# Odd tokens of two batches moved out of phase H0 and Y0, sums and kv by 64x64 quadrants, phi(q) ahead of phi(k)

## The chip, the cores and the metric

The kernel runs on one core of one Trainium2 chip. The metric is the device time of one execution in microseconds (us), taken from the runs listed below. A core has five engines that run side by side, each through its own list of instructions in order: TensorE (PE in the profile; its weight loads are shown as PEld), VectorE (DVE), ScalarE (ACT), GpSimd (POOL) and SyncE (SP). SP, ACT and POOL also start transfers (DMAs); those started by SP and ACT go through hardware queues, those started by POOL through a software queue, and all of them are carried by the same 16 DMA engines.

## What is computed

Linear attention over 8 batches, 8 heads, 576 tokens and 64 values per head, and behind it a two-layer network with a swish between its layers. Cut to what matters:

```python
def phi(x): return np.where(x > 0, x, np.exp(x) - 1.0) + 1.0
q_p, k_p = phi(q), phi(k)
kv  = np.einsum('bhsd,bhse->bhde', k_p, v)
z   = np.sum(k_p, axis=2)
num = np.einsum('bhsd,bhde->bhse', q_p, kv)
den = np.einsum('bhsd,bhd->bhs', q_p, z)[..., None] + 1e-06
x   = (num / den)            # heads put side by side: 4608 tokens x 512
h   = x @ w_in               # 512 -> 2048
g   = h / (1 + np.exp(-beta * h))
out = g @ w_out              # 2048 -> 512
```

## The kernel before

**Stages.** The order of all instructions is written out by hand; no scheduler changes it. For each block of tokens there is an H phase (h = x @ w_in, 16 column groups `ff` of four 512-column matmuls each, L395, and a Silu on ACT behind each group, L403) and a Y phase (out = g @ w_out, four row groups `t`, each of 16 matmuls in four parts `i`, L413). Phase H0/Y0 is batch 0, H1/Y1 batch 1, and so on to H7/Y7; a ninth pair, H8/Y8, takes what is left over from all batches, as follows.

**Odd tokens.** A batch has 576 tokens, held as J = 9 slices of 64. Eight slices make four blocks of 128 tokens (t = 0 to 3), which are the 512 tokens of a main phase. The ninth slice (t = 4, "odd") has 64 tokens; those of the eight batches are put side by side in `xT_tail` (512 columns), which only H8 reads, at the end of the kernel. For batches 2 to 7 the odd tokens are computed along with the others, in `numers` and `norms`. For batches 0 and 1 they have steps of their own: a transpose of their q (`q_trans` with t = 4), their denominators (`dens`, `recips`), their numerators (`numer0(b, 4)`) and a transpose of the quotient (`x_trans(b, 4, ...)`). Batch 0 has these four steps inside H0, after ff = 5, 7, 8 and 10 (L651 to L660); batch 1 has them in Y0 (L698, L703, L705), at its end (L736), and in H1 after ff = 8 (L778).

**Sums and kv of batches 0 and 1.** `row_products` (L175) multiplies a 64-row half of phi(k), all 128 columns, by a moving operand: two columns of ones for the sums z (`z_products`), 128 columns of v for kv (`kv_direct`). Half of each 128x128 product belongs to two different heads and is not wanted; `z_evac` and `kv_evac` multiply it away with a 0/1 mask while they copy it from PSUM. For batches 2 to 7 `kv_both` (L215) computes the same by 64x64 quadrants: four matmuls, one for each pair of a 64-row half and a 64-column half, that use different quarters of the array.

**Attention of batch 1.** It is worked into Y0. DVE and ACT do phi(k) first and phi(q) second (`phi_all`, L680 and L681: two exponentials on ACT, two relu steps and two minima on DVE for each). PE has Y0's parts i = 0 and 1 for all four t (32 matmuls, L682 to L684), two matmul groups more, the sums of batch 1, then the transposes of phi(q) in two lots with `y_mm` calls between them, kv, the denominators, and from L706 on the last parts of Y0 alternating with numerators and transposes.

**Loads.** POOL's queue loads, in this order: k of batch 0, v of batch 0, `w_in` (four parts), `w_out` parts 0 to 2, k of batch 1, q of batch 1, `w_out` part 3, v of batch 1, then q, k and v of batch 2 (L99 to L119, L517 to L522, L673 to L675). Batch 0's q is loaded in two halves by two hardware queues, SP's and ACT's (L93, L94). SP's queue also carries the stores of the output, the transposes made by DMA (`q_trans_dma`, `x_trans_dma`) of batches 2 to 7, and v of batches 3 to 7.

**PSUM and buffers.** `num0ps` and `miscps` have two banks each in the first part and are given up for `numps` before H1; `mmps` has four banks, which the H and Y phases turn through. phi(q) has two buffers (batch b uses the one of batch b - 2), and so has the tag `kv_bd`.

Of the kernel before, what the change touches and what calls it, by code (L numbers as in the profile page):

```python
# [8 lines left out]
F32 = mybir.dt.float32  # L9
BF16 = mybir.dt.bfloat16  # L10
ALU = mybir.AluOpType
# [5 lines left out]
def kernel(  # L17
# [72 lines left out]


    beta_row = consts.tile([FC, P], F32)
    for h0, eng in ((0, nc.sync), (2, nc.scalar)):  # L93
        load(eng, q0f, q, 0, h0, 2)  # L94
    nc.sync.dma_start(out=beta_row, in_=moe_beta.rearrange("(c p) -> c p", p=P))
    nc.vector.memset(warm, 0.5)  # L96
    tiny = consts.tile([P, 2], BF16)
    nc.scalar.activation(tiny[:, 0:1], warm[:, 0:1], ACTF.Exp)
    for h0 in (0, 2):  # L99
        load(nc.gpsimd, xk[0], k, 0, h0, 2)  # L100
# [15 lines left out]
    w_in_v = moe_w_in.rearrange("(c p) f -> p c f", p=P)  # L116
    w_out_v = moe_w_out.rearrange("(c p) m -> p c m", p=P)
    for i in range(4):
        nc.gpsimd.dma_start(out=w_in_sb[i], in_=w_in_v[:, :, i * 512 : (i + 1) * 512])  # L119

    def load_w_out(i):
        nc.gpsimd.dma_start(out=w_out_f[i], in_=w_out_v[:, i * 4 : (i + 1) * 4, :])
# [49 lines left out]
            vaug[b % 2][:, pr, :, :, 0:D], src[:, places(b, pr)].rearrange("p h j d -> p j h d")  # L172
        )

    def row_products(b, pr, dsts, mov):  # L175
        for j in range(J):
            for hh in range(2):
                r = slice(hh * G, (hh + 1) * G)
                nc.tensor.matmul(  # L179
                    dsts[hh], st[b, "k"][r, pr, j, :], mov(r, j),  # L180
                    start=(j == 0), stop=(j == J - 1), skip_group_check=True,
                )

    def z_products(b, pr, ps):

        row_products(b, pr, [a[:, 256 + 2 * pr : 258 + 2 * pr] for a in ps], lambda r, j: ones[r])

    def z_evac(ps):
        for hh in range(2):
            nc.vector.tensor_mul(  # L190
                z0[:, hh], ps[hh][:, 256:260].rearrange("p (a h) -> p a h", a=2),
                kvmask[:, :, :, 0],
            )

    def kv_direct(b, pr, ps):
        row_products(
            b, pr, [a[:, pr * P : (pr + 1) * P].rearrange("p (h d) -> p h d", h=2) for a in ps],
            lambda r, j: vb[b][r, 2 * pr : 2 * pr + 2, j, :],
        )

    def kv_evac(b, hh, prs, ps):
        p0, p1 = prs[0], prs[-1] + 1
        nc.vector.tensor_mul(
            st[b, "kv"][:, hh, p0:p1].rearrange("p a (h e) -> p a h e", h=2)[:, :, :, 0:D],
            ps[hh][:, p0 * P : p1 * P].rearrange("p (a h d) -> p a h d", a=p1 - p0, h=2),
            kvmask[:, p0:p1, :, 0:D],
        )

# [6 lines left out]
    def kv_both(b):  # L215

        t = num_tile("kvp")
        for pr in range(2):
            for j in range(J):
                for h in range(2):  # L220
                    for hh in range(2):
                        r = slice(hh * G, (hh + 1) * G)
                        c = slice(h * D, (h + 1) * D)
                        nc.tensor.matmul(  # L224
                            t[c, hh, pr * EA : (pr + 1) * EA],
                            st[b, "k"][r, pr, j, c],
                            vaug[b % 2][r, pr, j, h, 0:EA],
                            start=(j == 0), stop=(j == J - 1), skip_group_check=True,
                        )
        st[b, "kvd"] = work.tile([P, 2, 2 * EA], BF16, tag="kv_bd", name="kvd")  # L230
        nc.vector.tensor_copy(st[b, "kvd"], t[:, :, 0 : 2 * EA])  # L231

# [15 lines left out]
    def q_trans(b, ts, tp, engs):  # L248

        if (b, "qT") not in st:  # L250
            st[b, "qT"] = work.tile([P, NT, 2, 2, P], BF16, tag="qT", name="qT")
        slots = 1 if ts[0] == NT - 1 else 2
        tv = tp.rearrange("p (t a h i g) -> p t a h i g", a=2, h=2, i=slots, g=G)
        for k, t in enumerate(ts):
            for pr in range(2):
                for i in range(slots):
                    nc.tensor.matmul(  # L257
                        tv[:, k, pr, :, i, :], st[b, "q"][:, pr, 2 * t + i, :], identity,
                        is_transpose=True, start=True, stop=True, skip_group_check=True,
                    )  # L260
        for k, (t, eng) in enumerate(zip(ts, engs)):
            q_copy(b, k, t, tp, eng)

    def q_trans_dma(b):
        st[b, "qTd"] = work.tile([P, 38, G], BF16, tag="qT", name="qTd")
        nc.gpsimd.memset(st[b, "qTd"][:, 36:37], 0.0)
        for hh in range(2):
            st[b, "qTd", "dma"] = nc.sync.dma_start_transpose(
                out=st[b, "qTd"][:, hh * 2 * J : (hh + 1) * 2 * J],
                in_=st[b, "q"][hh * G : (hh + 1) * G].rearrange("p a j c -> p (a j c)"),  # L270
            )

    def q_stat(b, t, hh, pr, n):
        if (b, "qTd") in st:
# [27 lines left out]
    def numers(b):  # L302
        pairs = [num_tile("nps") for _ in range(2)]
        odd = [mm_tile("nps_m") for _ in range(2)]
        for k in range(2):
            dst = [pairs[k][:, h] for h in range(2)]
            numer_tile(b, dst, k)
            numer_tile(b, dst, 2, (k,), 4)
        numer_tile(b, odd, 3)
        for hh in range(2):  # L310
            quads(b, odd, 4 + hh, lambda c: (c, J - 1), hh, None)
        st[b, "nps"] = pairs, odd

    def xs_tile(b, t):
        st[b, "xs", t] = work.tile([P, 8, D], BF16, tag="xs", name="xs", bufs=4)
# [45 lines left out]
    def x_trans(b, t, eng):  # L361
        n = P if t < NT - 1 else G
        xv = st[b, "xs", t].rearrange("p i a d -> p (i a d)")
        if b == 1 and t == NT - 1:
            tp = num_tile("xtp")[:, 0].bitcast(BF16)[:, 0 : KC * P].rearrange(
                "p (c t) -> p c t", c=KC
            )
        else:
            tp = miscps.tile([P, KC, P], BF16, tag="misc", name="xtp")
        for p in range(KC):  # L370
            nc.tensor.matmul(  # L371
                tp[:, p, :n], xv[:n, p * P : (p + 1) * P], identity[:n, :n],
                is_transpose=True, start=True, stop=True, skip_group_check=True,
            )
        if eng is nc.scalar:
            nc.scalar.copy(x_dst(b, t), tp[:, :, :n])
        else:
            eng.tensor_copy(x_dst(b, t), tp[:, :, :n])  # L378

    def x_trans_dma(b, t):  # L380
# [4 lines left out]

        for pr in range(2):
            nc.sync.dma_start_transpose(
                out=xT_tail[:, pr:4:2, b * G : (b + 1) * G],
                in_=xv[pr * G : (pr + 1) * G, 0 : 2 * P],
            )  # L390

# [155 lines left out]
    bps = miscps.tile([P, FC], F32, tag="misc", name="bps")  # L547
    nc.tensor.matmul(bps, beta_row, ident16, is_transpose=True, start=True, stop=True)
    nc.scalar.copy(beta_s, bps)
    z_evac(zt)  # L550

    def q_trans0(t):
        q_trans(0, (t,), misc_bf()[:, 0 : 512 if t < NT - 1 else 256], (nc.scalar,))

    def numer_part(ts, pr):
        numer_norm(ts, pr, numer_mm(ts, pr))
# [55 lines left out]
    def diagonal(hh):  # L612

        for h in range(2):
            r = slice(h * D, (h + 1) * D)
            nc.scalar.copy(
                kv0[r, hh, 1, h * EA : h * EA + D], kvp0[hh][r, P + h * D : P + (h + 1) * D]
            )

    diagonal(0)  # L620
# [26 lines left out]
    for ff in range(4, FC):  # L647
        hp = mm_tile("h_ps")
        h_mm(0, xT[0], ff, hp)
        silu(0, ff, hp)  # L650
        if ff == 5:  # L651
            q_trans0(4)
        if ff == 7:
            dps4 = num0_tile()
            dens(0, (4,), dps4)
            recips(4, 5, G, dps4)
        if ff == 8:
            numer0(0, 4)
        if ff == 10:
            x_trans(0, 4, nc.vector)  # L660

    def w_out_scale(i, n_act):
        for c in range(4):
# [13 lines left out]
    for i in range(3):  # L677
        w_out_scale(i, 0)
    yps = [mm_tile("y_ps") for _ in range(4)]
    phi_all(1, "k")  # L680
    phi_all(1, "q")  # L681
    for i in range(2):  # L682
        for t in range(4):
            y_mm(0, t, i, yps[t])  # L684
    kv1 = [miscps.tile([P, 512], F32, tag="misc", name="kv1") for _ in range(2)]
    kv_tile(1)
    y_mm(0, 0, 2, yps[0])
    y_mm(0, 1, 2, yps[1])
    for pr in range(2):
        z_products(1, pr, kv1)  # L690
    z_evac(kv1)
    w_out_scale(3, 0)
    y_mm(0, 2, 2, yps[2])
    for ts in ((0, 1), (2, 3)):
        q_trans(1, ts, num0_tile().bitcast(BF16), (nc.scalar, nc.scalar))
    y_mm(0, 3, 2, yps[3])
    dps1 = num0_tile()
    q_trans(1, (4,), dps1.bitcast(BF16)[:, 512:768], (nc.scalar,))  # L698
    for pr in range(2):
        kv_direct(1, pr, kv1)  # L700
    for hh in range(2):
        kv_evac(1, hh, (0, 1), kv1)
    dens(1, range(NT), dps1)  # L703
    recips(0, 4, P, dps1)
    recips(4, 5, G, dps1)  # L705
    y_mm(0, 0, 3, yps[0])  # L706
    y_out(0, 0, yps[0], copier=nc.scalar)
    numer0(1, 0)
# [24 lines left out]
    for pr in range(2):  # L733
        phi_relu(2, "k", pr, xin(2, "k", pr))
        phi_min(2, "k", pr)
    numer0(1, 4)  # L736
    num0_pool.__exit__(None, None, None)
    misc_pool.__exit__(None, None, None)
    numps = ctx.enter_context(tc.tile_pool(name="numps", bufs=2, space=bass.MemoryType.PSUM))
# [33 lines left out]
    for b in range(1, B + 1):  # L773
        n = b + 1
        sh, sy = {}, {}
        if b == 1:
            at(sh, 0, lambda: q_trans_dma(2))
            at(sh, 8, lambda: x_trans(1, 4, nc.vector))  # L778
            at(sh, 1, lambda: [v_copy(nc.gpsimd, 2, pr) for pr in range(2)])
            at(sh, 2, lambda: load_kq(3, st[2, "qTd", "dma"]), lambda: load_v(3))  # L780
        if n < B:
            at(sh, 10, lambda: kv_both(n))
            at(sh, FC - 1, lambda: numers(n), lambda: [norms(n, k) for k in range(3)])
# [40 lines left out]
```

## Time and profile before

| what | value | from |
|---|---|---|
| median of 3 runs | 290.11 us (290.07 to 290.31) | the times |
| the profiled execution, whole | 290.31 us | the times |
| its span in the profile | 288.5 us | the page |
| PE busy | 279.8 us, 97% of the span | the page |
| ACT, DVE, POOL busy | 159.7, 107.2, 36.7 us | the page |
| H0 with 512 columns starts (L395) | 20.66 us | the chain of waits |
| Y0 starts (L413) | 32.40 us | the chain of waits |
| H1 starts | 52.16 us | the chain of waits |
| Y1, H2, Y2 start | 68.00, 81.92, 97.28 us | the chain of waits |

The profiled execution is the slowest of the three; 290.31 less 288.5, 1.8 us, lies outside the span. All moments in the text are counted from the start of the span. The chain of waits follows the work that ended last back to the start: at each step to the instruction, or the transfer, that released it. What stands in the chain sets the end; what does not stand in it was hidden behind something. A line of the timeline reads: start, duration, engine, line of the code, operation, what it writes and reads, count, and in brackets how long the engine stood idle before and what released it. PE's durations in the timeline overlap (its work is pipelined), so what a group of matmuls adds to the time is read from the chain, where the pieces do not overlap.

### The profile page before, as it was taken

How to read it: one execution, taken by the hardware profiler on the slowest of the kernel's cores; microseconds unless marked ns; L12 is line 12 of the kernel's file. 1: busy time of each engine (PE TensorE's matmuls, PEld its weight loads, DVE VectorE, ACT ScalarE, POOL GpSimd, SP SyncE). 2: the span in 40 equal slices, each digit the busy share in tenths (PEclk: the TensorE clock that was granted, in tenths of full speed). 3: DMA queues.
4: the chain of work that ended last, by engine and by line, in shares of the span. 5: the costliest groups of instructions: out<-in, count | busy, mean ns of one | idle time of the engine just before them, and what ended most of it. 6: DMA issues, size and time to landing. Idle time of an engine off the chain costs nothing.

```text
span 288.5 us, 5796 instructions
## 1 busy us (share of the span) xinstructions
PE 279.8 (97%) x2409; PEld 137.3 (48%) x2409; DVE 107.2 (37%) x261; ACT 159.7 (55%) x217; POOL 36.7 (13%) x54
## 2 busy tenths in 40 slices
PE   7799999999999999999999999999999999999994
PEld 2574457544444444444444444544454444444443
DVE  3842776825710581048103920393025100110021
ACT  4777757966647843685277628771750186028400
POOL 8632100320014000400050007000000000000000
PEclk9999999999999999999999999999999999999999
DMA  7999999599499739973898489749304410230033
GB/s 215 206 218 395 247 252 204 124 208 209 79 150 287 127 69 157 282 134 65 136 272 156 78 147 272 141 82 136 93 2 78 116 36 0 65 82 1 0 75 74
DMA packets 51083, 40.90 MB, mean 142 GB/s; under 512 B 30944, under 2 KB 42480, under 8 KB 51056
## 3 DMA queue, kind: packets, MB, share of 16 engines
q1 hardware_dynamic: 37888, 22.89, 37.0%
q0 software_dynamic: 12736, 16.91, 29.7%
q10 hardware_dynamic: 432, 0.72, 0.7%
q8 instruction: 19, 0.31, 0.4%
q14 instruction: 8, 0.07, 0.1%
HBM read 36.71 MB, written 9.44 MB: 160 GB/s over the span
## 4 chain that ended last, share of the span: by engine, by line
PE 93%; DVE 2%; DMA 2%; ACT 1%; issue 0%; DVEq 0%
PE y_ps L413 43%; PE h_ps L395 42%; DMA stage<-in_q_dram 2%; PE kvp L224 1%; PE h_ps L597 1%; PE nps L289 1%; PE kv L179 1%; DVE phi_q L153 1%; PE nps_m L289 1%; PE xtp L371 0%; PE nps L493 0%; ACT e L142 0%; DVE r L146 0%; PE tp L587 0%; PE nps L257 0%
## 5 line engine op out<-in xcount | busy, mean ns | idle before, releaser
L403 ACT ACTIVATE g<-h_ps,beta_c 128x512 bf16<-128x512 f32 x144 | 98.0, 688 | 95.9 <-PE h_ps L395 95.4
L413 PE MATMUL y_ps<-w_out,g 128*128 128x512 bf16 (+3 forms) x600 | 127.1, 371 | 0.0
L395 PE MATMUL h_ps<-xT,w_in 128*128 128x512 bf16 x496 | 110.2, 379 | 0.3 <-DVE xT L378 0.2
L413 PEld LDWEIGHTS <-g 128*128 128x128 bf16 x600 | 57.6, 98 | 64.0
L395 PEld LDWEIGHTS <-w_in 128*128 128x128 bf16 x560 | 53.9, 98 | 63.9 <-issue 0.2
L237 DVE COPY y_sb<-y_ps 128x512 f32<-128x512 f32 (+2 forms) x35 | 23.4, 672 | 73.3 <-PE y_ps L413 73.3
L231 DVE CAST kvd<-kvp 128x260 bf16<-128x260 f32 x6 | 2.6, 428 | 50.0 <-PE kvp L224 50.0
L83 POOL DMA_DIRECT2D xq<-in_q_dram x7 | 5.2, 744 | 110.5 <-ACT g L403 75.9
L142 ACT ACTIVATE e<-xk 128x1152 bf16<-128x1152 bf16 x16 | 17.7, 1149 | 0.0
L142 ACT ACTIVATE e<-xq 128x1152 bf16<-128x1152 bf16 x14 | 15.6, 1155 | 0.1
L395 PE MATMUL h_ps<-xT_tail,w_in 128*128 128x512 bf16 x64 | 14.0, 379 | 0.0
L153 DVE TENSOR_TENSOR phi_k<-e,r 128x1152 bf16<-128x1152 bf16 x16 | 11.6, 751 | 2.2 <-ACT e L142 2.0
L319 DVE TENSOR_TENSOR xs<-nps,rden 128x512 bf16<-128x512 f32 (+1 forms) x24 | 12.2, 552 | 0.4
L153 DVE TENSOR_TENSOR phi_q<-e,r 128x1152 bf16<-128x1152 bf16 (+2 forms) x17 | 11.6, 717 | 0.7 <-ACT e L142 0.4
L328 DVE TENSOR_SCALAR den<-nps 128x12 f32<-128x12 f32 x12 | 2.0, 164 | 25.8 <-PE nps L289 25.8
L171 POOL CAST vaug<-vf 128x1152 bf16<-128x1152 f32 x10 | 11.2, 1157 | 1.8 <-DMA vf<-in_v_dram 1.8
L142 ACT ACT_TABLE_LOAD x6 | 7.7, 1283 | 2.8 <-DMA xq<-in_q_dram 1.7
L131 PE MATMUL warm_ps<-xT 128*128 128x512 bf16 x20 | 7.2, 524 | 1.5 <-DVE xT L96 1.5
L319 DVE TENSOR_TENSOR xs<-nps_m,rden 128x256 bf16<-128x256 f32 (+1 forms) x24 | 7.3, 351 | 3.2 <-DMA xT<-xs 3.0
L403 ACT ACT_TABLE_LOAD x6 | 7.7, 1283 | 0.1
L83 POOL DMA_DIRECT2D xk<-in_k_dram x9 | 6.8, 751 | 3.7 <-DMA g<-in_moe_w_out_dram 2.4
L146 DVE TENSOR_SCALAR r<-xk 128x1152 bf16<-128x1152 bf16 x16 | 6.8, 453 | 0.6 <-DMA xk<-in_k_dram 0.6
(86 smaller groups left out, 122.5 us busy)
## 6 DMA issues: line engine op xcount, KB each, us to landing
out_dram<-y_sb SPq DMA_DIRECT2D x70, 128.0 KB, 2.4
vf<-in_v_dram SPq DMA_DIRECT2D x5, 1152.0 KB, 6.5
xk<-in_k_dram POOLq DMA_DIRECT2D x7, 576.0 KB, 12.5
xq<-in_q_dram POOLq DMA_DIRECT2D x7, 576.0 KB, 10.2
w_in<-in_moe_w_in_dram POOLq DMA_DIRECT2D x4, 512.0 KB, 12.8
g<-in_moe_w_out_dram POOLq DMA_DIRECT2D x2, 1024.0 KB, 18.3
stage<-in_moe_w_out_dram POOLq DMA_DIRECT2D x2, 1024.0 KB, 20.8
vf<-in_v_dram POOLq DMA_DIRECT2D x2, 576.0 KB, 21.5
```

What stands on the lines that cost most here:

```text
L83: return eng.dma_start(out=dst[:, h0 : h0 + n].rearrange("p h j d -> p h (j d)"), in_=rows.rearrange("(i p) e -> p i e", p=P)[:, h0 : h0 + n],
L131: nc.tensor.matmul(warm_ps[:, 0:cols], warm[:, 0:P], warm[:, 0:cols], start=True, stop=True)
L142: nc.scalar.activation(st[b, a, pr, "e"][:, :, j0:j1], x[:, :, j0:j1], ACTF.Exp)
L146: nc.vector.tensor_scalar(r, x, 0.0, 1.0, ALU.max, ALU.add)
L153: nc.vector.tensor_tensor(st[b, a][:, pr, j0:j1].rearrange("p j (h d) -> p j h d", h=2), st[b, a, pr, "e"][:, :, j0:j1].rearrange("p h j d ...
L171: eng.tensor_copy(vaug[b % 2][:, pr, :, :, 0:D], src[:, places(b, pr)].rearrange("p h j d -> p j h d"))
L237: eng.tensor_copy(dst, src)
L289: nc.tensor.matmul(dst[h][c * G : (c + 1) * G, e * EA : (e + 1) * EA], st[b, "qTd"][r, (hh * 2 + p) * J + j, :], st[b, "kvd"][r, hh, p * E ...
L319: nc.vector.tensor_mul(out, num, rd[..., None].to_broadcast(list(num.shape)))
L395: nc.tensor.matmul(hp[:, c0:c1], w_in_sb[ff // 4][:, kc, (ff % 4) * P : (ff % 4 + 1) * P], x[:, kc, c0:c1], start=(kc == 0), stop=(kc == K ...
L403: nc.scalar.activation(g_sb[b % 2][:, ff, :], hp, ACTF.Silu, scale=beta_c[:, ff : ff + 1])
L413: nc.tensor.matmul(yp[:, c0:c1], g_sb[b % 2][:, ff, t * P : (t + 1) * P], w_out_sb[i][:, c, c0:c1], start=(ff == 0), stop=(ff == FC - 1), ...
```

## The change

Five edits, all of them in one diff:

- Both halves of batch 0's q are loaded by SP's queue.
- Sums and kv of batches 0 and 1 are computed by quadrants (`k_quads`), which replaces `row_products`; `z_evac` also copies z into the 65th columns of the batch's kv tile, on POOL.
- The odd tokens of batches 0 and 1 leave H0, Y0 and H1. Their q is transposed by eight small DMAs on SP's queue (`q_odd_dma`): those of batch 0 held until the last part of `w_in` has landed, those of batch 1 after ff = 4 of H1. Numerators and denominators of both batches are computed in H2 after ff = 10, by 16 quadrant matmuls (`odd_numers`, `odd_norms`), and their quotients transposed by four DMAs after ff = 11.
- Batch 1: phi(q) comes before phi(k); the two lots of transposes of phi(q) come ahead of the sums; the sums follow Y0's part i = 2 and kv follows them directly; `w_out_scale(3)` on DVE stands ahead of the mask steps.
- The memset of one unused column in `q_trans_dma` goes, and two buffers are cut to what is used.

```diff
-    for h0, eng in ((0, nc.sync), (2, nc.scalar)):
-        load(eng, q0f, q, 0, h0, 2)
+    for h0 in (0, 2):
+        load(nc.sync, q0f, q, 0, h0, 2)
...
-    def row_products(b, pr, dsts, mov):
+    def k_quads(b, pr, dst, mov):
         for j in range(J):
-            for hh in range(2):
-                r = slice(hh * G, (hh + 1) * G)
-                nc.tensor.matmul(
-                    dsts[hh], st[b, "k"][r, pr, j, :], mov(r, j),
-                    start=(j == 0), stop=(j == J - 1), skip_group_check=True,
-                )
+            for h in range(2):
+                for hh in range(2):
+                    r = slice(hh * G, (hh + 1) * G)
+                    c = slice(h * D, (h + 1) * D)
+                    nc.tensor.matmul(
+                        dst[hh][c], st[b, "k"][r, pr, j, c], mov(r, j, h),
+                        start=(j == 0), stop=(j == J - 1), skip_group_check=True,
+                    )
...
-    def z_evac(ps):
+    def z_evac(b, ps):
...
+        nc.gpsimd.tensor_copy(
+            st[b, "kv"].rearrange("p x a (h e) -> p (x a h) e", h=2)[:, :, D],
+            z0.rearrange("p x a h -> p (x a h)"),
+        )
...
     def q_trans_dma(b):
-        nc.gpsimd.memset(st[b, "qTd"][:, 36:37], 0.0)
...
+    def q_odd_dma(b, after=None):
+        for hh in range(2):
+            for pr in range(2):
+                d = nc.sync.dma_start_transpose(
+                    out=q_odd[b][:, 2 * hh + pr, :],
+                    in_=st[b, "q"][hh * G : (hh + 1) * G, pr, J - 1, :],
+                )
+                if after is not None:
+                    hold(d, after)
...
+    def odd_numers():
+        dst = num_tile("nps_o")
+        for b in range(2):
+            for hh in range(2):
+                for pr in range(2):
+                    for h in range(2):
+                        r = slice(h * D, (h + 1) * D)
+                        e = 2 * b + hh
+                        nc.tensor.matmul(
+                            dst[pr * G : (pr + 1) * G, h, e * EA : (e + 1) * EA],
+                            q_odd[b][r, 2 * hh + pr, :],
+                            st[b, "kv"][r, hh, pr, h * EA : (h + 1) * EA],
+                            start=True, stop=True, skip_group_check=True,
+                        )
+        st["odd"] = dst
+
+    def odd_norms():
+        nv = st["odd"][:, :, 0 : 4 * EA].rearrange("p h (n e) -> p h n e", e=EA)
+        den = work.tile([P, 2, 4], F32, tag="den", name="den")
+        rden = work.tile([P, 2, 4], F32, tag="rden", name="rden")
+        nc.vector.tensor_scalar(den, nv[:, :, :, D], 1e-6, None, ALU.add)
+        nc.vector.reciprocal(rden, den)
+        for b in range(2):
+            x = xs_tile(b, 4)[:, 0:4].rearrange("p (h n) d -> p h n d", h=2)
+            n = slice(2 * b, 2 * b + 2)
+            scale(x, nv[:, :, n, 0:D], rden[:, :, n])
...
     for ff in range(4, FC):
         hp = mm_tile("h_ps")
         h_mm(0, xT[0], ff, hp)
         silu(0, ff, hp)
-        if ff == 5:
-            q_trans0(4)
-        if ff == 7:
-            dps4 = num0_tile()
-            dens(0, (4,), dps4)
-            recips(4, 5, G, dps4)
-        if ff == 8:
-            numer0(0, 4)
-        if ff == 10:
-            x_trans(0, 4, nc.vector)
+    q_odd_dma(0, w_in_load)
...
     yps = [mm_tile("y_ps") for _ in range(4)]
+    phi_all(1, "q")
     phi_all(1, "k")
-    phi_all(1, "q")
     for i in range(2):
         for t in range(4):
             y_mm(0, t, i, yps[t])
     kv1 = [miscps.tile([P, 512], F32, tag="misc", name="kv1") for _ in range(2)]
     kv_tile(1)
+    q_trans(1, (0, 1), num0_tile().bitcast(BF16), (nc.scalar, nc.scalar))
     y_mm(0, 0, 2, yps[0])
     y_mm(0, 1, 2, yps[1])
+    q_trans(1, (2, 3), num0_tile().bitcast(BF16), (nc.scalar, nc.scalar))
+    w_out_scale(3, 0)
+    y_mm(0, 2, 2, yps[2])
+    y_mm(0, 3, 2, yps[3])
     for pr in range(2):
         z_products(1, pr, kv1)
-    z_evac(kv1)
-    w_out_scale(3, 0)
-    y_mm(0, 2, 2, yps[2])
-    for ts in ((0, 1), (2, 3)):
-        q_trans(1, ts, num0_tile().bitcast(BF16), (nc.scalar, nc.scalar))
-    y_mm(0, 3, 2, yps[3])
-    dps1 = num0_tile()
-    q_trans(1, (4,), dps1.bitcast(BF16)[:, 512:768], (nc.scalar,))
+    z_evac(1, kv1)
     for pr in range(2):
         kv_direct(1, pr, kv1)
     for hh in range(2):
         kv_evac(1, hh, (0, 1), kv1)
-    dens(1, range(NT), dps1)
+    dps1 = num0_tile()
+    dens(1, range(4), dps1)
     recips(0, 4, P, dps1)
-    recips(4, 5, G, dps1)
...
-    numer0(1, 4)
...
         if b == 1:
             at(sh, 0, lambda: q_trans_dma(2))
-            at(sh, 8, lambda: x_trans(1, 4, nc.vector))
...
+            at(sh, 4, lambda: q_odd_dma(1))
+        if b == 2:
+            at(sh, 10, odd_numers, odd_norms)
+            at(sh, 11, lambda: [x_trans_dma(i, 4) for i in range(2)])
```

## The prediction

> **What bounds the kernel now.** I read the page first, then the chain of waits from H0 to H1, then the timeline of ACT and POOL and the landing of two loads. The page names the engine, the chain its stretches:
>
> ```profile
> PE 279.8 (97%) x2409; PEld 137.3 (48%) x2409; DVE 107.2 (37%) x261; ACT 159.7 (55%) x217; POOL 36.7 (13%) x54
> ...
> PE 93%; DVE 2%; DMA 2%; ACT 1%; issue 0%; DVEq 0%
> ```
>
> PE's work is 93% of the chain, so a matmul taken out of it is time won, as long as PE does not then wait for something else. The chain through H0's rest and Y0 (start, duration, engine, tile, line, count):
>
> ```profile
> 22.55 0.11 PE tp L257 x2
> ...
> 24.39 0.22 PE nps L475 x4
> ...
> 25.58 0.35 PE nps L493 x4
> ...
> 27.76 0.22 PE xtp L371 x4
> 27.98 4.42 PE h_ps L395 x20
> 32.40 8.63 PE y_ps L413 x40
> 41.04 0.54 PE kv L179 x36
> ...
> 44.42 1.11 PE kv L179 x36
> 45.53 0.70 PE nps L475 x20
> ...
> 62.14 0.71 PE kvp L224 x72
> ```
>
> The left-out lines are more h_ps and y_ps, the transposes of batch 1's q (16 in 0.89, the odd two in 0.12) and H1's odd transpose (60.09, 0.22). PE stands nowhere in Y0 until 51.66. But what feeds it there is tight. ACT's timeline, and the two loads with their issue and their time to landing (last column of the transfer view):
>
> ```profile
> 34.09 1.28 ACT L142 ACT_TABLE_LOAD   x1 [0.96 <-DMA xk<-in_k_dram]
> 35.38 2.22 ACT L142 ACTIVATE e<-xk 128x1152 bf16<-128x1152 bf16 x2
> 37.50 2.20 ACT L142 ACTIVATE e<-xq 128x1152 bf16<-128x1152 bf16 x2
> ```
>
> ```profile
> 12.13 0.75 POOL L83 DMA_DIRECT2D xk<-in_k_dram  x1 [0.34 <-DMA vf<-in_v_dram]
> 14.66 0.75 POOL L83 DMA_DIRECT2D xq<-in_q_dram  x1 [1.78 <-DMA w_in<-in_moe_w_in_dram]
> ```
>
> ```profile
> xk<-in_k_dram POOLq DMA_DIRECT2D x1, 576.0 KB, 21.9
> xq<-in_q_dram POOLq DMA_DIRECT2D x1, 576.0 KB, 22.2
> ```
>
> k of batch 1 lands at 12.13 + 21.9 = 34.03, and ACT, idle for 0.96 us, starts on it at once. q of batch 1 lands at 14.66 + 22.2 = **36.86**, 2.83 us later. The order k, q on ACT and DVE is the order of landing. From 6 to 48 us the window view has the DMA engines busy throughout (share 1.02 to 1.27): a landing there is a place in a full queue.
>
> **Parts that shorten PE's list.** From the chain, where a duration is what the group adds:
> - H0: the odd steps of batch 0, 0.11 + 0.22 + 0.35 + 0.22 = 0.90.
> - Start: the first `kv_direct`, 18 matmuls, 0.65 in the chain; as 36 quadrants at the 0.71 / 72 = 9.9 ns of the L224 row 0.36, so 0.29 less. The second lies behind the reciprocals of DVE. The two q halves on one queue let the first land sooner and the second a little later; k's landing (exponentials from 7.97) holds the gain under about 0.5. I take 0.
> - Y0: transpose of the odd q 0.12; denominators 20 to 16, 0.70 x 4/20 = 0.14; kv 1.11 to 72 x 9.9 ns = 0.71, so 0.40. The sums go from 36 matmuls in 0.54 to 72 quadrants with one column, a form the trace lacks. At least 0.43 by full weight loads with two columns (L475 in batch 0: 16 in 0.39, 24 ns each, four quadrants being one load, so 18 of them), at most 0.71 by L224's 65 columns. I take 0.60, nearest L224, the same quadrants: 0.06 more. The odd numerators (L493 at 51.57) lie in the wait for DVE's copy of xT (51.66 to 52.16): worth nothing.
> - H1: the odd transpose, 0.22.
> - H2: 16 quadrants more, 16 x 9.9 ns = 0.16 (0.1 to 0.4 with switches of form).
>
> Without a new wait: 0.90 + 0.29 + 0.12 + 0.14 + 0.40 - 0.06 + 0.22 - 0.16 = 1.85 us won.
>
> **The step that costs.** `phi_all(1, "q")` now comes first on ACT and DVE, but POOL's order of loads is untouched: k still ahead of q. ACT's table load, DVE's relu and everything of phi(k) behind them wait for 36.86 instead of 34.03. And PE now wants phi(q) earlier: directly after the 32 matmuls of i = 0 and 1, where before phi(k) was wanted after 40.
>
> *When PE gets there.* 32 matmuls at 8.63 / 40 = 0.216 are 6.90: before, 32.40 + 6.90 = 39.30. With H0 and the start 1.19 shorter: 38.11.
>
> *When phi(q) is there.* In the trace, landing of k at 34.03, second minimum of phi(k) done at 38.39 (start 37.63, 0.76 long), PE 0.05 later as after other minima: 4.41 from landing to PE. q has the same instructions (1.15 an exponential, for k and for q). Then 36.86 + 4.41 = 41.27, the first half about 1.05 earlier. PE waits some **3.2 us**, and everything gained ahead of that is only more waiting.
>
> *What moves the landing.* The eight new DMAs: those of batch 0 go out when the last `w_in` part lands (23.1; POOL's load at 23.14 was released by w_in), 64 KB in four issues of 1.2 to 2.2 us on SP, which has nothing else until 47.85. So they run inside the full stretch ahead of q. By the qTd transposes (two, 288 KB, DMA share 0.91 over 55.8 to 60.0, some 3.7 us) 64 KB take 0.83 us of all engines; by xT (128 KB, 0.67) 0.34. I take 0.5. Below nothing: one queue might empty q of batch 0 sooner, into the unused share of 1.5 to 3.5 us (0.46 to 0.94, worth 0.5 us). So -0.5 to 0.8, and PE resumes at 41.27 + 0.50 = 41.77.
>
> *From there to H1.* 6 remaining transposes 0.33, eight matmuls 0.97 + 0.86 = 1.83, eight transposes 0.45, eight matmuls 1.72, sums 0.60, kv 0.71, denominators 0.56; then as before from 46.23 to 52.16, 5.93. Sum 12.13: H1 at 53.90, against 52.16, **1.74 later**. With H1 (-0.22) and H2 (+0.16): 1.68 us. Against the profiled execution 290.31 + 1.68 = 291.99; that one is 0.20 above the median of its runs, so I say **291.8**.
>
> **What is late next.** phi(k) follows phi(q): its exponentials end about 36.86 + 0.5 + 0.06 + 1.29 + 4.42 = 43.1, DVE's last minimum 44.0, the sums want it at 46.1. `w_out_scale(3)` behind it on DVE (1.66) ends 45.7, ahead of the mask steps at 46.7 and of part i = 3 at 48. ACT's four copies of q (0.5 each) start when its exponentials end at 43.1 and are done by 46. Each has 0.7 us or more; if not, H1 moves by the shortfall.
>
> **Moves at no cost, and their cover.** SP: the four issues of batch 1's odd q (1.2 to 2.2 us) fall in its idle stretch 60.9 to 68.8; if they overrun by 0.9, the xT transposes behind them still land about 5 us ahead of H2 (their four issues ended at 75.05 before, H2 starts at 81.92). The four of H2, 4.8 us from about 94, end near the first xT issue (98.11); H3 reads xT at 111.2. DVE: `odd_norms`, by rows L328, L329 and L319 0.16 + 0.23 + 2 x 0.35 = 1.1 us, stands ahead of the copy of kvp (0.43), which PE wants 4.42 us later. POOL: two copies of 8 columns against six memsets (0.16 to 0.32 each); behind them only loads that wait longer for landings and a copy for 62 us.
>
> [...] In the trace the clock shows in spacing: the warm-up matmuls follow at 0.43 us until 6.1 us and at 0.216 in Y0, though the granted clock reads 1.00 in both. No row shows PE idle for over 0.9 us after that, so the price of the new wait on the clock is open here: nothing, or half speed until the rate returns, up to the 4.9 us that it took at the start (2.4 us lost).
> [...]
>
> **Rivals.**
> 1. *Faster, no wait.* If q lands early enough, 1.85 is won: 290.31 - 1.85 - 0.20 = 288.3. The mechanism would be a queue that is not full, so that q's landing is not bound to its place. It decides by the landing: no change in time where q lands 1.68 us ahead of my 37.36, at 35.7; the full gain from about 33.7. For it: the start's unused share. Against it: 22.2 us in the queue, share above 1. Chance 0.10.
> 2. *Wait and slow clock.* As forecast plus 1.2 to 2.4: 293.0 to 294.2. For it: 3.7 us is four times the longest wait of the trace. Against it: no row shows that a wait costs speed, and two transposes break this one. Chance 0.10.
> 3. *The small wait.* q lands about 1.2 to 1.7 us sooner than I say and the terms cancel: 290.0 to 290.6. Chance 0.04.
> The forecast has the remaining 0.76.
>
> **How the numbers follow.** Own range of the forecast: landing -1.0 / +0.3 about my 0.5, sums -0.17 / +0.11, H2 -0.06 / +0.24, other sums 0.1 each way: 290.5 to 292.6 with all ends together. With part of rival 2: 290.8 to 293.0. A measurement of this kernel tells 0.2%, 0.6 us, from no change. Faster takes rival 1; same takes rival 3 and the forecast's low tail (under 290.7), 0.06; slower the rest, 0.84.
>
> **What would show it.** The page after: ACT's first table load in Y0 released by xq instead of xk, near 37; PE idle 2.5 to 4 us ahead of the transposes of nps in Y0, released by DVE phi_q; that wait among the longest of PE; H1 near 53.9, and later phases of 13.9 us as before. Wrong if q lands before 35.7, if PE's wait is under 1.5 us, or if H1 starts before 52.

## The result, and the profile after

| | before | after |
|---|---|---|
| median (all runs) | 290.09 us (290.04 to 290.31) | 294.42 us (293.02 to 295.06) |
| ratio, with its 95% interval | | 1.0141 [1.0104, 1.0178] |
| profiled execution, its span | 290.31, 288.5 us | 294.29, 292.5 us |
| H1 starts | 52.16 us | 55.62 us |
| H2 starts | 81.92 us | 86.86 us |
| Y2 starts | 97.28 us | 102.41 us |

The change makes the kernel 1.4% slower, by 4.3 us. The direction is the predicted one; the size is more than twice the predicted 1.7 us, and 294.42 lies above the range. From the page of after: the busy times, PE's instruction queue, and the shares of the chain of waits:

```profile
PE 278.7 (95%) x2541; PEld 136.2 (47%) x2541; DVE 106.3 (36%) x257; ACT 159.7 (55%) x215; POOL 36.4 (12%) x50
...
q8 instruction: 20, 0.33, 0.4%
...
PE 81%; DMA 13%; POOL 1%; DVE 1%; issue 1%; ACT 1%; POOLq 0%; ACTq 0%; DVEq 0%
```

PE is 1.1 us less busy, in a span that is 4.0 us longer. PE's share of the chain falls from 93% to 81% and that of transfers rises from 2% to 13%: the kernel now waits for data, in two places. (The chain counts a transfer from its issue on: the 13% are 9.13, 22.24 and 7.42 us of transfers, in which PE mostly had other work. What PE waited is 3.0 and 1.60 us.) Both stand in the chain of after (start, duration, engine, tile, line, count):

```profile
14.70 22.24 DMA xq<-in_q_dram
...
38.30 2.22 ACT e L145 x2
40.55 0.77 DVE phi_q L156
41.36 0.51 PE nps L263 x6
41.87 2.69 PE y_ps L451 x8
44.57 0.85 PE nps L263 x8
45.42 2.02 PE y_ps L451 x8
47.44 0.75 PE kv L185 x72
48.25 0.17 DVE z L196
48.47 0.83 PE kv L185 x72
49.30 0.48 PE nps L513 x16
...
55.62 9.66 PE h_ps L433 x44
...
71.99 7.42 DMA xT<-xs
79.44 0.30 DVE xs L362
79.78 7.08 PE y_ps L451 x32
```

**The first wait** is the predicted one. q of batch 1 lands at 14.70 + 22.24 = 36.94, and PE resumes at 41.36. ACT's timeline names the releaser, with the idle time before it in brackets:

```profile
37.01 1.28 ACT L145 ACT_TABLE_LOAD   x1 [5.11 <-DMA xq<-in_q_dram]
```

**Behind it PE is slow.** Eight matmuls of 512 columns add 2.69 us, where eight at full speed add 8 x 0.216 = 1.73. The window view of after has the reason (stretch, length, busy time of PE, PEld, DVE, ACT and POOL, then the granted clock, DMA share, GB/s):

```profile
40.00:42.00 2.00, 0.92 (x10) 0.63 (x11) 1.71 (x5) 2.00 (x3) 0.00 (x0) 1.00 1.20 206
42.00:44.00 2.00, 2.00 (x8) 0.72 (x7) 2.00 (x5) 1.58 (x3) 0.00 (x0) 0.62 1.22 210
44.00:46.00 2.00, 2.00 (x13) 1.24 (x12) 1.00 (x3) 0.54 (x2) 0.00 (x0) 0.53 1.20 206
46.00:48.00 2.00, 2.00 (x79) 1.10 (x78) 0.00 (x0) 0.53 (x2) 0.00 (x0) 1.00 1.22 209
```

The trace's record of the clock gives one stretch at half rate, 42.48 to 45.90, 3.41 us long; it begins 1.1 us after PE goes on. Before has none between 6 us and the last stores; its window view of the same time:

```profile
42.00:44.00 2.00, 2.00 (x23) 1.41 (x22) 1.42 (x4) 0.97 (x3) 0.00 (x0) 1.00 1.20 205
44.00:46.00 2.00, 2.00 (x57) 1.64 (x56) 0.43 (x2) 1.35 (x4) 0.00 (x0) 1.00 1.22 211
```

**The second wait** is new and stands in Y1. In DVE's timeline the step that makes the quotient of the odd tokens waits for 4.55 us and ends at 79.9; before, the same step waited 1.87 us and began at 73.58, and PE did not notice. DVE after, DVE before, and PE after:

```profile
79.44 0.49 DVE L362 TENSOR_TENSOR xs<-nps_m,rden 128x128 bf16<-128x128 f32 x2 [4.55 <-DMA xT<-xs]
```

```profile
73.58 0.49 DVE L319 TENSOR_TENSOR xs<-nps_m,rden 128x128 bf16<-128x128 f32 x2 [1.87 <-DMA xT<-xs]
```

```profile
79.78 1.47 PE L451 MATMUL y_ps<-w_out,g 128*128 128x512 bf16 x6 [1.60 <-DVE xs L362]
```

DVE writes this quotient (t = 4) into the buffer that held t = 0's, and must let the transposes of t = 0 finish. Until then its numerators hold a PSUM bank that Y1 needs at t = 2, and PE stands for 1.60 us.

Against before, then: H1 starts 3.46 later; H1 with Y1 is 1.48 longer (31.24 against 29.76); H2 is 0.19 longer (15.55 against 15.36); Y2 with H3 is 0.55 shorter, of which 0.44 is a stop of PE that only before has (below); what follows the last row group, mainly the last stores, is 0.6 shorter. Sum 4.0, the difference of the spans.

### The profile page after: what moved, and what is told of

The parts are those of the page before. It is cut to its first block, busy times and chain, and to the rows that moved or that the text cites. A ratio compares the mean times of both kernels' runs of the same rounds, so it can differ in the third digit from the quotient of the medians.

```text
span 292.5 us, 6073 instructions
## 1 busy us (share of the span) xinstructions
PE 278.7 (95%) x2541; PEld 136.2 (47%) x2541; DVE 106.3 (36%) x257; ACT 159.7 (55%) x215; POOL 36.4 (12%) x50
## 4 chain that ended last, share of the span: by engine, by line
PE 81%; DMA 13%; POOL 1%; DVE 1%; issue 1%; ACT 1%; POOLq 0%; ACTq 0%; DVEq 0%
PE y_ps L451 39%; PE h_ps L433 38%; DMA xq<-in_q_dram 8%; DMA w_in<-in_moe_w_in_dram 3%; DMA xT<-xs 3%; PE kvp L185 1%; PE nps L304 1%; ACT e L145 1%; POOL vf L83 1%; PE kv L185 1%; PE nps L263 0%; POOL xk L83 0%; DVE xs L362 0%; PE nps L531 0%; PE xtp L409 0%
## 5 line engine op out<-in xcount | busy, mean ns | idle before, releaser
L451 PE MATMUL y_ps<-w_out,g 128*128 128x512 bf16 (+3 forms) x600 | 128.5, 373 | 1.6 <-DVE xs L362 1.6
L185 PEld LDWEIGHTS <-phi_k 64*64 64x64 bf16 x720 | 7.0, 107 | 4.6 <-issue 3.4
L134 PE MATMUL warm_ps<-xT 128*128 128x512 bf16 x20 | 6.5, 483 | 1.5 <-DVE xT L96 1.5
L149 DVE TENSOR_SCALAR r<-xq 128x1152 bf16<-128x1152 bf16 x14 | 5.8, 450 | 3.8 <-DMA xq<-in_q_dram 3.8
```

Of the source, the lines that this page charges most:

```text
L134: nc.tensor.matmul(warm_ps[:, 0:cols], warm[:, 0:P], warm[:, 0:cols], start=True, stop=True)
L149: nc.vector.tensor_scalar(r, x, 0.0, 1.0, ALU.max, ALU.add)
L185: nc.tensor.matmul(dst[hh][c], st[b, "k"][r, pr, j, c], mov(r, j, h), start=(j == 0), stop=(j == J - 1), skip_group_check=True,)
L451: nc.tensor.matmul(yp[:, c0:c1], g_sb[b % 2][:, ff, t * P : (t + 1) * P], w_out_sb[i][:, c, c0:c1], start=(ff == 0), stop=(ff == FC - 1), ...
```

## The experiments

The theory after the result had three terms: the late q, the half rate behind the wait, and the late quotient in Y1. A fourth showed itself on the way. Each ratio is to the kernel before, with runs of before taken alongside; a ratio above 1 is slower. e1 to e5 start from the changed kernel.

### e1_q_lands_first: take the wait for q away

```diff
-    load(nc.gpsimd, xk[1], k, 1)
     load(nc.gpsimd, xq[1], q, 1)
+    load(nc.gpsimd, xk[1], k, 1)
```

> The changed kernel with one edit: POOL loads q of batch 1 ahead of k of batch 1. Theory (PE's wait in Y0 is the landing of q, and the slow matmuls behind it follow from that wait): q lands near 34 instead of 36.94, phi(q) is there at 38.4, PE waits at most 0.5 us instead of 3.0, the matmuls of part i = 2 are at full speed, H1 starts near 51.3 instead of 55.62, and the time falls by about 4.3 to 289.5 to 290.5, with the wait of 1.6 us in Y1 still there. Rival A (phi(q) first is dear for another reason, the order on ACT and DVE): no more than 1 us better, 293.4 or more. Rival B (the wait in Y1 comes from the later start of H1 and not from the added transposes): the wait in Y1 goes as well, 288.0 to 288.8.

291.34 us (291.19 to 291.70), ratio 1.0050 [1.0033, 1.0067]. q lands at 35.43, PE's wait falls from 3.0 to 1.0 us, there is no half rate in Y0, and H1 starts at 52.58: 3.1 us of the 4.3 come from q's place in the queue. But it is still slower than before, and 0.8 us more than expected. PE's wait in Y1 is there still (1.1 us) though H1 starts only 0.4 later than before, so rival B, the later H1 as its cause, falls. And the half rate has moved to the start. The window view of e1_q_lands_first:

```profile
12.00:14.00 2.00, 1.83 (x61) 1.50 (x61) 1.14 (x5) 1.14 (x4) 0.86 (x2) 0.70 1.24 206
14.00:16.00 2.00, 1.86 (x16) 1.40 (x17) 0.87 (x3) 1.31 (x6) 0.75 (x1) 0.50 1.24 208
```

PE is busy for nine tenths of both stretches, with a clock of 0.70 and 0.50.

### e2_clock_held: leave the wait, fill it

```diff
     kv_tile(1)
+    fill = num0_tile()
+    for _ in range(10):
+        nc.tensor.matmul(fill, w_in_sb[0][:, 0, 0:P], w_in_sb[0][:, 0, :], start=True, stop=True)
     q_trans(1, (0, 1), num0_tile().bitcast(BF16), (nc.scalar, nc.scalar))
```

> The changed kernel with ten dummy matmuls of 512 columns (2.2 us) on PE ahead of the first transposes of phi(q) in Y0, inside its wait; nothing else moves. Theory (the half rate from 42 to 46 us follows from PE standing idle): the spacing of the matmuls of part i = 2 stays 0.216, H1 starts about 1.5 us earlier, near 54.1, time 292.5 to 293.1. Rival (the rate falls for another reason, or PE's wait is too broken to count): spacing 0.43 again, time 294.0 to 294.8.

292.60 us (292.35 to 293.16), ratio 1.0093 [1.0078, 1.0108], as expected. q lands later still (37.76), yet H1 starts at 54.77, 0.85 ahead of the changed kernel. The chain of e2_clock_held, for the matmuls that took 2.69 us:

```profile
42.69 1.73 PE y_ps L451 x8
```

That is full speed. So the half rate behind the wait is a cost of its own, 1.6 us in the changed kernel's profile (0.96 + 0.40 + 0.30 more for the three groups that it covers), and it comes of PE's standing still. The other profiles agree: Y0 has a half-rate stretch in the three in which PE stood there for 2.0 us or more at a time (after 2.23, e5 2.0, e8 2.23), and none in the other eleven, where no stand in Y0 was over 0.8. This kernel, too, has one half-rate stretch in the start (14.60 to 18.01).

### e3_odd1_in_y0 and e4_both: the odd transposes out of H1

e3 issues batch 1's four odd transposes in Y0 instead of H1; e4 does that and e1's edit.

```diff
     phi_all(1, "q")
+    q_odd_dma(1)
     phi_all(1, "k")
...
-            at(sh, 4, lambda: q_odd_dma(1))
```

> The changed kernel with the four transposes of batch 1's odd q issued in Y0, as soon as phi(q) is there, instead of after ff = 4 of H1. Theory (in H1 they take DMA time from the loads of batch 3, which then collide with the xT transposes, on which DVE and behind it PE wait in Y1): the xT transposes land within 3.5 us, DVE's wait for xT falls from 4.6 to under 2.5 us, PE's wait of 1.6 us in Y1 goes, time 292.5 to 293.1. Rival (the wait in Y1 comes from the later H1, with loads and transposes shifted against each other): DVE's and PE's waits stay, 294.0 to 294.8.

> Both edits: q of batch 1 loaded ahead of k, and batch 1's odd q transposed in Y0. Theory: both waits go, what the change takes out of PE's list is left: 288.0 to 288.9, faster than the kernel before. Rival (a third cost that neither edit touches): 289.5 or more.

e3: 292.82 us (291.43 to 294.20), ratio 1.0095 [1.0065, 1.0126]. The time is the expected one, but not for the expected reason: PE still waits 0.8 us in Y1, as in e2, where the odd transposes are in H1, and DVE still waits 3.75 us for the transposes of xT. The half rate, in this profile, lies in the start (17.70 to 21.12) and not in Y0. e4: 290.83 us (290.40 to 292.55), ratio 1.0035 [1.0018, 1.0052], against an expected 288.0 to 288.9: its rival, a third cost, is right. Its Y1 still has 1.1 us of PE's wait, DVE waits 4.05 us, and 6.83 us of its start run at half rate. The theory that the odd transposes make xT late falls as it stood: DVE's wait is 4.55, 4.01 and 3.75 us and PE's wait in Y1 1.6, 1.1 and 0.8 us with them in H1 (after, e1, e2), and 3.75 and 4.05, 0.8 and 1.1 without (e3, e4).

The transfer view shows part of what the xT transposes stand behind: POOL's loads of q and k of batch 3. From the first issue of xT on, these fill the engines (share 1.13 to 1.18) for 2.3 us in before (0.45 MB, against 0.01 MB on SP's queue), for 4.4 us in after and e1 (0.79 and 0.85 MB) and for 2.9 us in e3 and e4 (0.55 and 0.58 MB). So without the odd transposes in H1 the loads are through 1.5 us sooner after that issue. Yet xT still lands 6.6 and 6.9 us after its issue, against 7.4 and 6.9 with them and 4.7 in before. What holds it then is not known.

### e5_xs4_own and e6_q_first_xs4: a buffer of its own for the late quotient

e5 gives t = 4 of batches 2 to 7 its own buffer, so that nobody waits for the transposes of t = 0, however late they are; e6 adds e1's order of loads.

```diff
-        x = xs_tile(b, 4)
+        x = st[b, "xs", 4] = work.tile([P, 4, D], BF16, tag="xs4", name="xs4", bufs=1)
```

> The changed kernel in which the odd tokens' quotient of batches 2 to 7 has a buffer of its own, so that DVE's last step of norms no longer waits until the first xT transpose of the same batch has read its buffer. Theory (PE's wait of 1.6 us in Y1 is this: xT transpose late, DVE waits for the buffer, PE for the PSUM bank behind it, whatever delays the transpose): the wait goes, 292.5 to 293.2. Rival (the late transpose is felt somewhere else next, at H2's start): 294 to 294.8.

> The same buffer, and q of batch 1 loaded ahead of k. Both waits gone: 291.34 less the 1.1 us that PE still waited in Y1, 290.0 to 290.5. What is then left against the kernel before must lie in the start (slow clock at 12 to 19 us). It is the base for the next two. Rival: 291 or more, the Y1 wait moved and did not go.

e5: 292.94 us (291.19 to 293.54), ratio 1.0088 [1.0058, 1.0118]; the wait in Y1 is gone from PE's waits and 1.5 us from the time. e6: 290.08 us (288.63 to 291.50), ratio 1.0001 [0.9984, 1.0018]. Both as expected. So two edits, a swap of two lines and one buffer, take back all 4.3 us. But e6 has neither of the two waits left and PE's shorter list, which the prediction priced at 1.85 us, and it only comes level with before. Where are these? A part is the clock: nine of e6's ten runs have a mean granted clock of 0.994 or less, and the profiled one, at 1.000, took 289.18 us.

### e7_two_queues and e8_rows_batch0: undo the start's edits

Both start from e6. e7 loads batch 0's q by two queues again; e8 computes batch 0's sums and kv by `row_products` again, instead of quadrants.

```diff
-    for h0 in (0, 2):
-        load(nc.sync, q0f, q, 0, h0, 2)
+    for h0, eng in ((0, nc.sync), (2, nc.scalar)):
+        load(eng, q0f, q, 0, h0, 2)
```

> e6_q_first_xs4 with q of batch 0 loaded by two queues again, as in the kernel before. Theory L (the earlier phi(q) leaves PE idle between the transposes of q and the sums of k, and this lets the clock fall in the start): full clock from 6 us on in the profile, the 512-column part of H0 starts by 20.8, time 289.0 to 289.7. Rival Q (the quadrants, which occupy the array for less, let it fall): half rate in the start as in e6, 290.0 to 290.5.

> e6_q_first_xs4 with sums and kv of batch 0 by row products, as in the kernel before; q of batch 0 stays on one queue. Theory Q: full clock in the start, 289.2 to 289.8. Theory L: half rate in the start as in e6, 290.0 to 290.6.

e7: 289.43 us (288.90 to 290.99), ratio 0.9992 [0.9972, 1.0011]: 0.65 better than e6 in the median, with overlapping spreads. Its part of H0 with 512 columns starts at 21.67, not by 20.8. It keeps a stop of PE in the start that the changed kernel (0.92 us, up to 16.34) and e6 (1.01 us) have too. From e7's timelines of PE and, in the second fence, ACT:

```profile
17.35 0.62 PE L632 MATMUL h_ps<-xT,w_in 128*128 128x128 bf16 x8 [1.01 <-ACT xT L626]
```

```profile
16.38 0.37 ACT L626 COPY xT<-tp 128x256 bf16<-128x256 bf16 x1 [0.31 <-PE tp L622]
```

ACT's copy, the releaser named, was done at 16.38 + 0.37 = 16.75, 0.6 us before PE moves. Something else held it.

e8: 292.63 us (292.37 to 293.56), ratio 1.0095 [1.0072, 1.0117]. It was to take 289.2 to 290.6 and is 2.5 us slower than e6. In the start it is better: no stop, and H0 with 512 columns starts at 19.69 instead of 20.91. But in Y0, far from the edit, PE stops for 2.23 us in the middle of the denominators, released by nothing ("issue"). So these two runs do not decide between theories L and Q, and the profiles cannot either: the starts of e6, e7 and e8 all have the full clock there (the clocks of all runs, in the last section, lean to Q). PE's timeline of e8_rows_batch0:

```profile
45.66 0.18 PE L534 MATMUL nps<-z,qT 128*128 128x2 bf16 x1
48.07 0.51 PE L534 MATMUL nps<-z,qT 128*128 128x2 bf16 x15 [2.23 <-issue]
```

**What holds PE.** One transfer starts at the beginning of that stop, on the queue q8 that the page calls "instruction". The trace has 19 of them of 16 KB in before and in e8, 20 in the changed kernel. Before has 2409 matmuls and as many weight loads, 4818 / 19 = 254 to a transfer; after 5082 / 20 = 254. So they bring PE's own instructions, in blocks of some 254, or 127 matmuls with their weight loads. And the odd stops of PE end some 2.3 us behind the start of one:

| kernel | q8 transfer starts | PE goes on | later by |
|---|---|---|---|
| after | 14.03 | 16.34 | 2.31 |
| e7_two_queues | 15.05 | 17.35 | 2.30 |
| e8_rows_batch0 | 45.68 | 48.07 | 2.39 |
| before (the stop in Y3's approach) | 124.49 | 126.90 | 2.41 |

In e1, e2, e3, e4, e6 and e7 one more, 0.2 to 0.5 us long, stands ahead of Y2 and ends 2.3 to 2.5 us behind its transfer. The last of the table is the 0.44 us that the chain of before names "issue":

```profile
126.34 0.13 PE nps_m L289 x12
126.47 0.44 issue
126.90 0.29 PE nps_m L289 x12
```

The theory (F): PE stands where it runs through a block in less time than the 2.3 to 2.4 us from the start of a transfer to PE's going on. 127 matmuls of 512 columns last 27 us (0.216 each), and the next block is there in time (before's waits have one stop named "issue" in 19 transfers). 127 quadrants last some 1.3 us (72 in 0.75), and then PE stands. At what point of a block the next one is asked for was not shown. Quadrants do batch 1's sums and kv in 1.58 us (0.75 + 0.83, after) against 1.65 (0.54 + 1.11, before), but with 144 matmuls instead of 72, and every added or removed instruction shifts which part of the kernel lies at the edge of a block.

### e9_rows_shift64, e10_two_queues_shift104, e11_shift_z_early, e12_rows_shift_z: move the edges of the blocks

e9 is e8 with 64 tiny matmuls in the warm-up, where PE has nothing to do, so that all later edges fall half a block earlier; e10 is e7 with 104.

```diff
-    idle(15)
+    for i in range(64):
+        hh = i % 2
+        r = c = slice(hh * G, (hh + 1) * G)
+        nc.tensor.matmul(
+            warm_ps[c, hh : hh + 1], warm[r, c], warm[r, 0:1],
+            start=True, stop=True, skip_group_check=True,
+        )
+    idle(11)
```

e11 is e10, and e12 is e9, with batch 1's sums ahead of `y_mm(0, 3, 2, yps[3])`, so that DVE's step z between sums and kv has four matmuls beside it:

```diff
-    y_mm(0, 3, 2, yps[3])
     for pr in range(2):
         z_products(1, pr, kv1)
     z_evac(1, kv1)
+    y_mm(0, 3, 2, yps[3])
```

> e8_rows_batch0 with 64 tiny quadrant matmuls more in PE's warm-up at the start (and 11 wide warm-up matmuls instead of 15), nothing else. [...] The stand of 2.23 us at 45.8 of e8_rows_batch0 is gone, the q8 transfer near 45.7 starts earlier, near 35 to 44, and the time falls by 2.2 us and more: 289.0 to 290.5. Rival (the stand has another cause at that place, such as the z copy or the buffers of dps): it stays, 2 us or so ahead of the denominators of batch 1, and the time is 292 to 293.5.

> e7_two_queues with 104 tiny quadrant matmuls more in PE's warm-up (and 9 wide ones instead of 15), nothing else. Theory F: the stand of 1.01 us at 16.3 to 17.35 moves or goes; H0 with 512 columns starts at 20.4 to 21.1 instead of 21.67, and the time is 288.4 to 289.2 where the clock holds. Rival (the stand at 16.3 is a wait for ACT's copy of xT, as the profile names it): it stays at its place with 0.8 to 1.1 us, and the time is 289.2 to 289.7.

> e10_two_queues_shift104 with batch 1's sums issued ahead of Y0's matmuls of part 2 and t = 3, so that DVE's mask step of z lies beside four matmuls. Theory: the wait of 0.4 us for DVE's z ahead of kv goes, and the time is 0.3 to 0.5 below e10_two_queues_shift104: 288.0 to 288.9. Rival: phi(k), which the sums then want 0.9 us earlier, is late, and the wait only moves: within 0.2 of e10_two_queues_shift104.

> e9_rows_shift64 with batch 1's sums issued ahead of Y0's matmuls of part 2 and t = 3, as in e11_shift_z_early. If the gains add up (the 0.4 us wait for DVE's z goes, and the four matmuls in the middle of the dense run leave the fetch more time): 288.4 to 288.8, some 1.4 us below before. Rival (what e11_shift_z_early won over e10_two_queues_shift104 was its clock, 1.000 against 0.994 in the profiled runs, and not the wait): within 0.2 of 289.02.

| kernel | median, all runs | ratio, 95% interval |
|---|---|---|
| e9_rows_shift64 | 289.02 (288.63 to 289.52) | 0.9961 [0.9947, 0.9975] |
| e10_two_queues_shift104 | 289.26 (288.60 to 291.08) | 0.9977 [0.9962, 0.9991] |
| e11_shift_z_early | 288.77 (288.40 to 288.96) | 0.9954 [0.9942, 0.9967] |
| e12_rows_shift_z | 288.81 (288.00 to 289.16) | 0.9938 [0.9915, 0.9960] |

e9 is 3.6 us faster than e8, by instructions that compute nothing. PE's timeline of e9_rows_shift64, at the place where e8 stopped:

```profile
44.42 0.83 PE L185 MATMUL kv<-vf,phi_k 64*64 64x64 bf16 x72 [0.36 <-DVE z L208]
45.19 0.55 PE L534 MATMUL nps<-z,qT 128*128 128x2 bf16 x16
45.60 1.02 PE L472 MATMUL y_ps<-w_out,g 128*128 128x512 bf16 x4
```

The sixteen denominators run in one piece, and the third q8 transfer, which began at 45.68 in e8, begins at 34.82, ten us ahead of the dense run. Theory F holds, its rival falls: neither z's copy nor the tile was touched. 2.2 us of the 3.6 are the stop; the rest is of the size of the half rate (e8's profile has a stretch from 49.28 to 52.70, e9's has none).

e10: the stop at 16.3 goes as expected; but its profiled execution has a half-rate stretch in the start instead (14.18 to 17.59), H0 with 512 columns starts at 21.76, not at 20.4 to 21.1, and the time is at the edge of what was expected. That point is a miss: the clock took what the stop gave back.

e11 and e12: the wait for z goes from PE's waits in both. The times move by -0.49 and -0.21 us with overlapping spreads; e11's expectation is met, e12's median sits on its rival's edge, so what the z edit alone is worth is not settled. Both beat before, by 1.3 us. e11 (batch 0 by quadrants) and e12 (by rows) agree, but they also differ in the queues for q of batch 0 and in the shift, so this alone does not price the quadrants of batch 0. e9 and e12 keep a small wait of PE in Y2 (0.6 and 0.2 us), behind the transposes of the moved odd quotients in H2: the first of e9's stands in its chain at 92.97 for 8.63 us.

## Why the prediction was right in direction and wrong in size

**Right: the step that costs.** The path was that of the trace: PE done with Y0's first 32 matmuls at 38.08 (said 38.11), the table load in Y0 released by xq at 37.01, PE back at 41.36 (said 41.77). From the one to the other that is 3.3 us (said 3.7), 3.0 of them idle. That everything gained ahead of the wait is only more waiting held too: H0 became shorter, and none of it reached H1. e1 shows the cause by undoing it.

**Luck: that 38.11 was met.** Two terms in it were off, in opposite ways. H0 became 1.2 us shorter (11.74 to 10.5), not 0.90: its 48 matmuls cost 10.84 in five pieces before and 10.5 in one piece after, and the sum had left these switches out. The start gave nothing instead of 0.29: H0 with 512 columns starts at 20.66 before and after. With quadrants and two queues it starts at 21.67 (e7), with quadrants and one queue at 20.91 (e6), both behind the stop of 1.01; with rows and one queue at 19.69 (e8), without it. So one queue for q, taken as 0 and held to be under 0.5, is worth 0.8 to 1.0 us there, the stop takes as much back, and no gain of the quadrants shows.

**Too high: the landing.** The eight added DMAs were to delay q by 0.5 us. In the profiled run it landed at 36.94 against 36.86 before. In other kernels with the same order of loads it landed between 36.9 and 37.9, so the price, if the added DMAs are all of it, is 0 to 1 us, and the estimate was no worse than the spread.

**Failed: "the price of the new wait on the clock is open here".** The forecast took it as nothing and gave the other end 0.10, because "two transposes break this one". They did not: six more transposes, sixteen matmuls and eight transposes were to take 0.33 + 1.83 + 0.45 + 1.72 and took 0.51 + 2.69 + 0.85 + 2.02, 1.74 us more, and e2 shows that filling the wait takes 1.6 of it away. The rival with the half rate (293.0 to 294.2) was the nearest of the cases. No run shows the lower end of its 1.2 to 2.4; what the runs showed is 1.6 to 1.74. With both ends of an unknown price in hand the middle should not have been its lower end. The prediction had seen that the granted clock's column alone would not tell; here it did.

**Failed: the cover of the odd transposes in H1.** That "the xT transposes behind them still land about 5 us ahead of H2" was measured to the reader of xT. Who else waits was not asked. The transposes also free the buffer that DVE wants for t = 4, behind which a PSUM bank and PE hang in Y1: 1.6 us, shown by e5. Before's trace had the warning, DVE's wait of 1.87 us for the same transposes. What makes them land later than before stays open in part: they stand behind the loads of batch 3 for 2.1 us longer than in before, without the odd DMAs in H1 for 0.6 longer, but e3 and e4 won nothing of DVE's wait by that.

**Mis-sized: from the wait to H1.** The sums took 0.75 against 0.60 and kv 0.83 against 0.71. Between them stands 0.28 us for DVE's z: the sums, z and kv were apart before, now kv follows at once and shares the PSUM tile that z reads. The prediction did not name this wait; e11 and e12 remove it. Denominators (0.48 against 0.56), H1 (-0.30 against -0.22 for its length) and H2 (+0.19 against +0.16) were right.

**Failed: the 1.85 us "without a new wait".** e6 has q at 34.7 and no wait in Y1. By the prediction's own terms q is then 2.66 us ahead of its 37.36, and 2.66 - 1.68 = 0.98 is won: 289.1. e6's median is 290.08; only its profiled run, at full clock, has 289.18. The sum priced matmuls by their time alone. Quadrants also cost instructions, and these come through the same full transfer engines (share 1.24 from 14.03 to 16.34 in after): 0.9 to 1.0 us of stop in the start, 0.2 to 0.5 ahead of Y2, up to 2.2 in Y0 (e8), and half-rate stretches in most runs. Only with the edges moved (e9, e11, e12) do 1.0 to 1.3 us appear in the median.

The range was too narrow because what the sum left out lies on one side: the slow clock (1.6), the late quotient (1.60) and the wait for z (0.28). The stop in the start did not add to the changed kernel's time, since it lies ahead of the wait for q.

## What to carry to other kernels

When an operand is wanted in another order, swap its loads too: here both loads landed some 22 to 23 us after their issue in either order (21.9 to 23.0), so the one wanted first has to be issued first. Where an added transfer stands ahead of others in a queue, ask not only who reads what lands late but who waits for the buffer that the late transfer still reads. Count instructions and not only time when work is cut into smaller matmuls, and look in the trace for stops of PE that end some 2.2 to 2.5 us behind the start of an instruction transfer.

## What the hardware showed

- **Half rate without an idle stretch.** All half-rate stretches read in the middle of these profiles are 3.41 us long or twice that. In e1 one began at 12.78; in the 3.41 us ahead of it PE was busy for 2.75, and its longest stand was 0.81. So the rate fell there without a long stand of PE, where in Y0 it fell behind stands of 2.0 us and more (after, e5, e8). In such starts PE's work is hundreds of quadrants, transposes and 1-column products with short gaps; that this work itself lets the rate fall is a guess, and which of the small waits decides was not tried. The mean clocks of the runs point to the quadrants of batch 0: with them and no long stand in Y0, 0.994 or less was read in 21 of 23 runs with one queue for q (e1, e4, e6) and in 14 of 26 with two (e7, e10, e11); with row products and no such stand, in 2 of 12 with one queue (e9, e12) and in 4 of 59 with two (before). The number of stretches differs from one execution to the next: e10's runs have mean clocks of 0.988 to 1.000 and go from 288.6 to 291.1 us; one stretch is 3.41 / 2 / 287 = 0.6% of the mean clock. The 4 of before's 59 runs took 291.2 to 291.6 us at 0.992 to 0.994; the others were at 0.996 or more.
- **PE can starve for its own instructions.** Its instructions came in transfers of 16 KB, some 254 to a transfer. With the transfer engines full (DMA share 1.24 from 14.03 to 16.34 in after, 0.99 from 124.49 to 126.90 in before) and quadrants of some 10 ns each, PE stood at some edges, for 0.2 to 2.23 us a stop. What an edge costs with idle engines is not shown here.
- **Small transposes by DMA landed late.** The eight odd ones, 16 KB each, took 6.4 us from issue to landing in the median, against 2.5 us for all those of xT. Four issues took 6.03 us on SP's queue in H1, about as long as xT's four (6.59). All eight ran beside large loads (DMA share 1.04 from 22.6 to 30 in after, 0.93 from 60 to 68, 1.25 from 68 to 75), so whether their size or the full engines made them slow is not shown.
